# Seven block products for eight in a token mixer's first channel product, for the last two of its five units

## The chip, the cores and the metric

The kernel runs on one core of a Trainium2 chip. The metric is the device time of one execution in microseconds. TensorE (PE) multiplies matrices into PSUM, VectorE (DVE) and ScalarE (ACT) work on SBUF and PSUM, GpSimd (POOL) on SBUF, and the queues of SyncE (SP) and ScalarE issue the DMAs.

## What is computed

```python
def _attn_ref(x, w_r, w_i, b_r, b_i):                # x: 8 x 3008 x 256
    X = np.fft.rfft(x, axis=1)
    Yr = Xr @ w_r - Xi @ w_i + b_r                   # Xr, Xi: real and imaginary part
    Yi = Xr @ w_i + Xi @ w_r + b_i
    ...                                              # both shrunk towards zero by 0.01
    return np.fft.irfft(Y, n=x.shape[1], axis=1)

def _moe_ref(x, w_tok1, w_tok2, w_ch1, w_ch2):
    h = np.maximum(xt @ w_tok1, 0.0) @ w_tok2        # over the 3008 tokens, 256 hidden
    u = x + h.transpose(0, 2, 1)
    h2 = np.maximum(u @ w_ch1, 0.0) @ w_ch2          # over the 256 channels, 1536 hidden
    return u + h2
```

The second function is applied to the result of the first.

## The kernel before

The eight batches are worked through in five units: batch 0, batch 1, and three pairs (`UNITS`, units 0 to 4). For each unit there are two kinds of work.

The spectral steps (`spectral`, `parts`) are the Fourier transform as dense matmuls: a transform of 47 points in 13 groups (`dft47`, `stage1`, which subtract and add pairs of rows first, in `sum_diff`), then for 12 pairs of frequencies a transform of 64 points (`forward`, tiles `px`, `xf`, `xth`, `xtl`), the complex product with the weights and the shrinking (`mix`, tiles `pm`, `z`, `yh`, `yl`), the way back (`inverse`, to `b_d` in DRAM) and the first token product, which adds up in `gp` (`tokens`). `close` rectifies `gp` into `gh` and `gl`, the inputs of the second token product.

The channel steps (`channel`) take a unit's tokens in chunks of 512 columns (the first of a pair's chunks has 384). `make_u` makes u for 470 or 376 tokens at once from `gh`, `gl`, the token weights (`wt2`, loaded by `load_wt2`) and the unit's `b_d` (`load_b2`); `split_u` splits a chunk of u. `first(f)` multiplies one of 12 blocks of 128 hidden values into a PSUM bank `ph` and rectifies it into `hh` and `hlo`; `second(f - 2)`, two blocks later, multiplies them into `po`, which holds the chunk's output through all 12 blocks.

All of these matmuls are made in a form of float32 that TensorE rounds, so each operand is held as a high part and a low part and each product is three matmuls, `mm3`:

```python
        PE.matmul(out, lhsT=wh, rhs=xh, start=start, stop=False)
        PE.matmul(out, lhsT=wh, rhs=xl, start=False, stop=False)
        PE.matmul(out, lhsT=wl, rhs=xh, start=False, stop=stop)
```

`split` makes the two parts: the high one is a copy (ScalarE, or VectorE for u), the low one a subtraction (VectorE, GpSimd in places). PSUM is eight banks: four go round under the tag `w` (`bank`), two belong to `po` and two to `gp`.

The order of the work around the change is written out by hand in the last loop. The channel chunks of unit u are run in turn, and between their blocks the loop takes steps of the spectral generator of unit u + 1, at a pace worked out from two sums of costs: 70.3 us for a batch of spectral steps (`left_s`) and 32.7 us for a channel chunk (`left_c`). At `"end"`, in the last chunk of a unit, what is left of the spectral steps is run. So unit 4's channel has no spectral steps beside it. A scheduler then puts each engine's instructions in order by what is ready in its own model, without changing what waits for what; engines run their queues in order.

Of the kernel before, what the change touches and what calls it, by code (L numbers as in the profile page):

```python
# [10 lines left out]
F32 = mybir.dt.float32  # L11
# [22 lines left out]
NCH = 1  # L34
NF = DF // 128


# [84 lines left out]
def tile_kernel(ctx: ExitStack, tc: tile.TileContext, io):  # L122
# [3 lines left out]
    const = ctx.enter_context(tc.tile_pool(name="const", bufs=1))  # L126
    wk = ctx.enter_context(tc.tile_pool(name="wk", bufs=2))
    dram = ctx.enter_context(tc.tile_pool(name="dram", bufs=1, space=bass.MemoryType.DRAM))
# [55 lines left out]

    def mm3(out, wh, wl, xh, xl, start, stop):
        PE.matmul(out, lhsT=wh, rhs=xh, start=start, stop=False)  # L186
        PE.matmul(out, lhsT=wh, rhs=xl, start=False, stop=False)  # L187
        PE.matmul(out, lhsT=wl, rhs=xh, start=False, stop=stop)  # L188


    f1w = const.tile([120, 3, 128], F32, name="f1")
    f1 = f1w[:, :, :120]
    f1r = const.tile([120, 2, 2, 128], F32R, name="f1r")
    f2 = const.tile([128, 4, 96], F32, name="f2")
# [3 lines left out]
    bias = const.tile([128, 2, C], F32, name="bias")  # L198
    wmh = const.tile([128, 3, 2, C], F32R, name="wmh")
    wml = const.tile([128, 3, 2, C], F32R, name="wml")  # L200
    wc = {}

# [18 lines left out]
    a_d = [dram.tile([128, KH, 512], F32, name=f"a_d{p}") for p in range(2)]  # L221
    b_d = [dram.tile([NSLOT, 96, 512], F32, name=f"b_d{p}") for p in range(2)]

# [177 lines left out]


    def parts(u):
        plain = u == 0
        bs = UNITS[u]
        nb = len(bs)
        w = nb * C
        a, bd = a_d[u % 2], b_d[u % 2]

# [111 lines left out]
        def close():  # L521
            gh = const.tile([128, 2, nb, C], F32R, name="gh", tag="gh")
            gl = const.tile([128, 2, nb, C], F32R, name="gl", tag="gl")
            for j in range(2):
                hv, gv = gh[:, j].rearrange("p b c -> p (b c)"), acc[0][:, j, :w]
                S.activation(out=hv, in_=gv, func=AF.Relu)
                V.scalar_tensor_tensor(out=gl[:, j].rearrange("p b c -> p (b c)"), in0=gv, scalar=0.0, in1=hv.bitcast(F32), op0=ALU.max, op1=ALU.subtract)
            gts[u] = gh, gl

        return SimpleNamespace(**{k: v for k, v in locals().items()})  # L530
# [49 lines left out]
    def begin(sp):  # L580
# [14 lines left out]
        with tc.tile_pool(name="early", bufs=1) as early:  # L595
# [25 lines left out]
            for n in range(NW + KP):  # L621
# [37 lines left out]
                if n in (NC + 9, NC + 10):  # L659
                    f.append(narrow_w2(len(f), early))  # L660
        wc["wk2"] = ctx.enter_context(tc.tile_pool(name="wk2", bufs=2))
        load_b2(0)
# [22 lines left out]
    for u, bs in enumerate(UNITS):  # L685
        total, at = N * len(bs), 0
        widths = [k * TOKS for k in sizes] if u == 0 else [total % CW] + [CW] * (total // CW)
# [21 lines left out]
    def load_wt2(g, pool=None):  # L709
        u, _, s, k = groups[g]  # L710
        cols = slice(s * TOKS, (s + k) * TOKS)
        if u == 0:
            wfs[g] = [load_wide(io["wt2"][0, jt][:, cols], k * TOKS, pool) for jt in range(2)]
        else:
            w = wk.tile([128, 4, 480], F32R, name="wt2", bufs=1)
            DMA.dma_start(out=w[:, :, :k * TOKS].bitcast(F32), in_=wt2_d[:, :, cols])
            wts[g] = w
# [11 lines left out]
    def load_b2(g):  # L729
        u, b, s, k = groups[g]  # L730
        b2 = wc["wk2"].tile([96, SPC, C], F32, name="b2", bufs=1)
        DMA.dma_start(out=b2[:, :k], in_=b_d[u % 2].rearrange("s q w -> q s w")[:, s:s + k, b * C:(b + 1) * C])
        b2s[g] = b2

    def make_u(g):
# [6 lines left out]
        for m in homes:  # L742
            if m not in ufs:
                ufs[m] = wc["wk2"].tile([128, 2, CW], F32, name="uf", bufs=3)
        for ct in range(2):
# [29 lines left out]
    def channel(n):  # L775
# [23 lines left out]
        for f in range(NF + 2):  # L799
# [9 lines left out]
            if after:  # L809
                mine = needs[n + 1]  # L810
                if f == 0 and mine:
                    load_wt2(mine[0])
                if f == 2:
                    if after[0] != u:
                        yield "end"
                    if mine:
                        load_b2(mine[0])
                first_at = 9 if len(mine) == 1 else 6
                for i, g in enumerate(mine):
# [7 lines left out]
                if f == 10:  # L827
                    split_u(n + 1)
            yield (1.37 if f in (0, 1, NF, NF + 1) else 2.73) * cw / CW
        o = wk.tile([128, 2, CW], F32, tag="o", name="o", bufs=3)  # L830
        step = 2 if after else 1
# [7 lines left out]


    def run(gen):
        for _ in gen:
            pass
# [68 lines left out]
```

## Time and profile before

| | |
|---|---|
| three runs | 2445.38, 2449.03 and 2450.14 us, median 2449.03 |
| profiled execution, first to last instruction (its span) | 2442.4 us |
| lowest of the runs less that span | 3.0 us |
| TensorE, VectorE, ScalarE, GpSimd busy | 2420.4, 1103.6, 875.3, 305.2 us |
| granted TensorE clock | 1.00 |

The time of the profiled execution outside its span is not shown apart; the three runs lie 3.0 to 7.7 us above the span. Busy times of TensorE come from matmuls that overlap, so the row of one matmul is longer than the distance to the next one's start.

### The profile page before, as it was taken

The numbers are of one execution on the slowest core, as the hardware profiler recorded it, in microseconds if no ns is written. First come the engines' busy times: TensorE is split into PE (matmuls) and PEld (weight loads), VectorE is DVE, ScalarE is ACT, GpSimd is POOL, SyncE is SP. The second block draws the span as 40 slices with busy tenths as digits, with TensorE's granted clock in tenths as the row PEclk, the third lists the DMA queues.
The fourth block names the chain that finished last, engine by engine and source line by source line (L and its number), as shares of the span: only waits on it lengthen the run. The fifth ranks groups of instructions, "written<-read, shape, count | busy, mean of one in ns | idle before, by whom it ended". The sixth has DMA issues, their size and how long they took to land.

```text
span 2442.4 us, 31613 instructions
## 1 busy us (share of the span) xinstructions
PE 2420.4 (99%) x12848; PEld 2114.3 (87%) x12848; DVE 1103.6 (45%) x1680; ACT 875.3 (36%) x1580; POOL 305.2 (12%) x259
## 2 busy tenths in 40 slices
PE   8999999999999999999999999999999999999999
PEld 7778999988888888888888898888888888888887
DVE  7986655454445444433344353444334333232332
ACT  6764444443333343333333253333333222222221
POOL 0000223122222011111111120111111000000000
PEclk9999999999999999999999999999999999999999
DMA  8864335542324352223322363232321212112110
GB/s 216 254 210 141 102 111 160 167 138 93 100 86 131 112 170 72 60 80 91 89 75 69 98 177 105 68 99 76 93 67 37 70 50 64 59 49 81 37 56 18
DMA packets 143998, 246.07 MB, mean 101 GB/s; under 512 B 10293, under 2 KB 97677, under 8 KB 143853
## 3 DMA queue, kind: packets, MB, share of 16 engines
q1 hardware_dynamic: 114073, 190.57, 26.4%
q10 hardware_dynamic: 29780, 53.49, 7.0%
q8 instruction: 101, 1.65, 0.3%
q14 instruction: 44, 0.36, 0.0%
HBM read 159.74 MB, written 84.28 MB: 100 GB/s over the span
## 4 chain that ended last, share of the span: by engine, by line
PE 93%; DMA 2%; DVE 2%; ACT 1%; SPq 1%; issue 0%; POOL 0%; ACTq 0%; DVEq 0%; POOLq 0%
PE ph L186 10%; PE ph L187 10%; PE ph L188 10%; PE po L188 10%; PE po L186 10%; PE po L187 10%; PE pu L751 5%; PE px L451 3%; PE pm L186 2%; PE pm L188 2%; PE pm L187 2%; PE pu L186 2%; PE pu L187 2%; PE pu L188 2%; PE gp L186 2%; PE gp L188 2%
## 5 line engine op out<-in xcount | busy, mean ns | idle before, releaser
L790 DVE SCALAR_TENSOR_TENSOR hlo<-ph,hh 128x512 fp32r<-128x512 f32 (+4 forms) x588 | 392.0, 667 | 640.0 <-ACT hh L789 635.8
L789 ACT ACTIVATE hh<-ph 128x512 fp32r<-128x512 f32 (+4 forms) x588 | 340.9, 581 | 822.3 <-PE ph L188 820.2
L186 PE MATMUL ph<-uh,w 128*128 128x512 f32 (+4 forms) x1176 | 455.7, 388 | 0.9 <-DVE hlo L790 0.9
L187 PE MATMUL ph<-ul,w 128*128 128x512 f32 (+4 forms) x1176 | 449.1, 382 | 0.0
L186 PE MATMUL po<-hh,w2h 128*128 128x512 f32 (+4 forms) x1176 | 448.5, 381 | 0.0
L188 PE MATMUL ph<-uh,w 128*128 128x512 f32 (+4 forms) x1176 | 448.5, 381 | 0.0
L187 PE MATMUL po<-hlo,w2h 128*128 128x512 f32 (+4 forms) x1176 | 447.9, 381 | 0.0
L188 PE MATMUL po<-hh,w2l 128*128 128x512 f32 (+4 forms) x1176 | 447.8, 381 | 0.0
L188 PEld LDWEIGHTS ph<-uh,w 128*128 128x128 f32 x1176 | 220.8, 188 | 39.5
L187 PEld LDWEIGHTS po<-hlo,w2h 128*128 128x128 f32 x1176 | 220.9, 188 | 38.6
L186 PEld LDWEIGHTS po<-hh,w2h 128*128 128x128 f32 x1176 | 220.8, 188 | 38.5
L188 PEld LDWEIGHTS po<-hh,w2l 128*128 128x128 f32 x1176 | 220.8, 188 | 38.4
L186 PEld LDWEIGHTS ph<-uh,w 128*128 128x128 f32 x1176 | 221.2, 188 | 35.5 <-DVE hlo L790 1.3
L187 PEld LDWEIGHTS ph<-ul,w 128*128 128x128 f32 x1176 | 221.3, 188 | 34.0 <-DVE ul L760 0.2
L140 DVE TENSOR_TENSOR xtl<-xf,xth 128x768 fp32r<-128x768 f32 x84 | 80.5, 958 | 208.7 <-ACT xth L137 208.7
L186 PE MATMUL pm<-wmh,xth 128*128 128x256 f32 x504 | 144.4, 287 | 1.1 <-ACT xth L137 1.1
L758 ACT COPY uf<-pu 128x470 f32<-128x470 f32 (+23 forms) x188 | 62.7, 376 | 228.1 <-PE pu L751 228.1
L140 POOL TENSOR_TENSOR yl<-z,yh 128x512 fp32r<-128x512 f32 x72 | 92.9, 1290 | 408.6 <-ACT yh L137 408.6
L188 PE MATMUL pm<-wmh,xtl 128*128 128x256 f32 x504 | 142.4, 283 | 0.0
L187 PE MATMUL pm<-wml,xth 128*128 128x256 f32 x504 | 142.3, 283 | 0.0
L751 PEld LDWEIGHTS pu<-g,b 96*128 96x128 f32 x1024 | 130.8, 191 | 3.4
L454 POOL TENSOR_TENSOR xf<-xf 128x256 f32<-128x256 f32 x84 | 69.0, 821 | 484.8 <-ACT xf L453 483.3
(130 smaller groups left out, 3216.3 us busy)
## 6 DMA issues: line engine op xcount, KB each, us to landing
wt<-wt_d SPq DMA_DIRECT2D x28, 940.0 KB, 5.6
x<-in_x SPq DMA_DIRECT2D x39, 480.0 KB, 4.4
a<-a_d SPq DMA_DIRECT2D x36, 512.0 KB, 3.8
b_d<-bt ACTq DMA_DIRECT2D x36, 512.0 KB, 3.3
out<-o SPq DMA_DIRECT2D x34, 512.0 KB, 2.8
a_d<-a ACTq DMA_DIRECT2D x36, 480.0 KB, 3.4
wt<-wt_d SPq DMA_DIRECT2D x21, 752.0 KB, 5.2
b<-b_d SPq DMA_DIRECT2D x32, 480.0 KB, 6.3
```

What stands on the lines that cost most here:

```text
L140: lo_eng.tensor_tensor(out=lo, in0=src, in1=hi.bitcast(F32), op=ALU.subtract)
L186: PE.matmul(out, lhsT=wh, rhs=xh, start=start, stop=False)
L187: PE.matmul(out, lhsT=wh, rhs=xl, start=False, stop=False)
L188: PE.matmul(out, lhsT=wl, rhs=xh, start=False, stop=stop)
L451: PE.matmul(pt[:, o:o + 128], lhsT=x, rhs=f2cols(2 * kp + ab), start=True, stop=True)
L454: (V if plain else G).tensor_tensor(out=xf[:, 0], in0=xf[:, 1], in1=xf[:, 2], op=ALU.add)
L751: PE.matmul(pt[:, s * TOKS:(s + 1) * TOKS], lhsT=b2[:, s, cs], rhs=g2[:, 0 if s0 + s == 0 else 1], start=False, stop=s == k - 1)
L758: S.copy(out=ufs[m][:, ct, lo - at:hi - at], in_=pt[:, lo - c0:hi - c0])
L789: S.activation(out=hh, in_=pt, func=AF.Relu)
L790: V.scalar_tensor_tensor(out=hlo, in0=pt, scalar=0.0, in1=hh.bitcast(F32), op0=ALU.max, op1=ALU.subtract)
```

## The change

Units 3 and 4 do the first channel product with seven block products in place of eight. A chunk has 1024 columns there (the first one 896), cut into two halves of 512 (448). The block matrix of weights has two hidden blocks by two blocks of 128 channels, that of u two blocks of channels by two halves. `weigh` makes four sums of weight blocks (`ws`), `sum_u` four sums of the blocks of u (in `t7`), `split_u7` splits the seven right factors (`ub`). `first7` makes the products of one pair of hidden blocks, into four banks: x takes three of them, w two, q and z one each. The results are read out between: what x and w hold after the first and second product is copied to SBUF by ScalarE (`snap`), and VectorE adds q, w and x to the copies. The four rectified blocks wait one pair for `second7`, which adds up both halves' outputs, in the two banks of `po` and the two of `gp`. So `gp` is no longer free for spectral steps beside them: those of units 3 and 4 stand beside unit 2's channel (`BESIDE`). `gh` and `gl` of units 3 and 4 go to DRAM in between (`g_d`), `b_d` has one copy for each unit, and the pools of the spectral steps are closed before the new tiles are opened (`open_seven`, in unit 2's last chunk).

```diff
+SEVEN = (3, 4)
+CW7 = 2 * CW
+BESIDE = {0: [1], 1: [2], 2: [3, 4]}
...
         def close():
-            gh = const.tile([128, 2, nb, C], F32R, name="gh", tag="gh")
-            gl = const.tile([128, 2, nb, C], F32R, name="gl", tag="gl")
+            if u in SEVEN:
+                gh, gl = hl([128, 2, nb, C], "gh"), hl([128, 2, nb, C], "gl")
+            else:
+                ...
             gts[u] = gh, gl
+            if u in SEVEN:
+                for i, g in enumerate(gts[u]):
+                    PUT.dma_start(out=g_d[u][i], in_=g.rearrange("p j b c -> p (j b c)").bitcast(F32))
...
+    def open_seven():
+        spectrum.close()
+        pool = wc["seven"] = ctx.enter_context(tc.tile_pool(name="seven", bufs=1, side="right", reuse_waits="tile"))
+        wc["wt2"] = wc["b2"] = wc["uf"] = pool
+        wc["ws"] = pool.tile([128, NF // 2, 4, 2, 128], F32R, name="ws")
...
+    def sum_u(n):
+        ...
+        b11, b12, b21, b22 = (uf[:, t, k * h:(k + 1) * h] for t in range(2) for k in range(2))
+        ...
+        V.tensor_tensor(out=t1, in0=b12, in1=b11, op=ALU.subtract)
+        V.tensor_tensor(out=t2, in0=b22, in1=t1, op=ALU.subtract)
+        V.tensor_tensor(out=t3, in0=b22, in1=b12, op=ALU.subtract)
+        V.tensor_tensor(out=t4_, in0=b21, in1=t2, op=ALU.subtract)
+        us[n] = uf, (b11, t1, b21, t2, b22, t4_, t3), []
...
+    def first7(n, p):
+        ...
+        product(x, 4, 0)
+        S.copy(out=snap[0], in_=x)
+        product(w, 0, 1)
+        S.copy(out=snap[1], in_=w)
+        product(q, 5, 2)
+        V.tensor_tensor(out=snap[0], in0=q, in1=snap[0], op=ALU.add)
+        product(x, 1, 3, False)
+        S.copy(out=snap[2], in_=x)
+        rectify(0, 0, snap[0])
+        product(w, 3, 4, False)
+        V.tensor_tensor(out=snap[2], in0=w, in1=snap[2], op=ALU.add)
+        rectify(0, 1, snap[2])
+        product(z, 6, 5)
+        S.copy(out=snap[3], in_=z)
+        product(x, 2, 6, False)
+        V.tensor_tensor(out=snap[3], in0=x, in1=snap[3], op=ALU.add)
+        V.tensor_tensor(out=snap[1], in0=x, in1=snap[1], op=ALU.add)
+        rectify(1, 0, snap[3])
+        rectify(1, 1, snap[1])
+        return hs
...
+    def channel7(ns):
+        ...
+        for n in ns:
+            ...
+            for p in range(half):
+                hs = first7(n, p)
+                if behind:
+                    second7(*behind, 0, (0, 1))
+                if p < len(mine):
+                    make_u(mine[p])
+                    ...
+                if behind:
+                    second7(*behind, 1, (0, 1))
+                    if p == 0:
+                        for k in range(2):
+                            finish7(behind[0], k, 2)
+                behind = n, p, hs
+                if after and p == half - 2:
+                    sum_u(after)
+                    for i in range(2):
+                        split_u7(after, i)
+                if after and p == half - 1:
+                    for i in range(2, 7):
+                        split_u7(after, i)
...
     for n, (u, at, cw) in enumerate(chunks):
-        if at == 0 and u + 1 < len(UNITS):
+        if u in SEVEN:
+            channel7(range(n, len(chunks)))
+            break
+        if at == 0:
             if u:
-                sp, done = spectral(u + 1), 0.0
-            left_s = len(UNITS[u + 1]) * 70.3 - done
+                sp, done = chain.from_iterable(spectral(v) for v in BESIDE[u]), 0.0
+            left_s = sum(len(UNITS[v]) for v in BESIDE[u]) * 70.3 - done
```

Up to the start of unit 2's channel every engine has the same instructions in the same order as before. The built order at three places, each with the waits that the instruction itself holds (`Activation` is ScalarE):

TensorE, unit 4's last chunk, before: one hidden block of `first` (`ph`), one of `second` (`po`).

```order
L186 MATMUL ph<-uh,w_949 128x512
L187 MATMUL ph<-ul,w_949 128x512
L188 MATMUL ph<-uh,w_949 128x512
L186 MATMUL ph<-uh,w_949 128x512
L187 MATMUL ph<-ul,w_949 128x512
L188 MATMUL ph<-uh,w_949 128x512
L186 MATMUL po<-hh,w2h 128x512 [waits Activation_49]
L187 MATMUL po<-hlo,w2h 128x512 [waits DVE_49]
L188 MATMUL po<-hh,w2l 128x512
L186 MATMUL po<-hh,w2h 128x512
L187 MATMUL po<-hlo,w2h 128x512
L188 MATMUL po<-hh,w2l 128x512
```

TensorE, unit 4's last chunk, now: the first four products of a pair of hidden blocks, x, w, q and x again (line 192 to 194 is `mm3`).

```order
L192 MATMUL sx<-ub,w_957 128x512 [waits DVE_49]
L193 MATMUL sx<-ub,w_957 128x512
L194 MATMUL sx<-ub,w_957 128x512
L192 MATMUL sw<-ub,ws 128x512 [waits DVE_49]
L193 MATMUL sw<-ub,ws 128x512
L194 MATMUL sw<-ub,ws 128x512
L192 MATMUL sq<-ub,w_957 128x512 [waits Activation_49]
L193 MATMUL sq<-ub,w_957 128x512
L194 MATMUL sq<-ub,w_957 128x512
L192 MATMUL sx<-ub,ws 128x512 [waits Activation_49]
L193 MATMUL sx<-ub,ws 128x512
L194 MATMUL sx<-ub,ws 128x512
```

Between a bank's filling and its next use there were other banks' blocks only; now the second product into x stands 6 matmuls behind the first, and waits for ScalarE's copy of it.

ScalarE, around a chunk border in unit 4, before: `hh` rectifies, `uf` is u copied from PSUM.

```order
L789 ACTIVATE hh<-ph 128x512 [waits DVE_49,PE_49] x12
L758 COPY uf<-pu 128x104 [waits PE_49]
L758 COPY uf<-pu 128x272
L758 COPY uf<-pu 128x104 [waits PE_49]
L758 COPY uf<-pu 128x272
L789 ACTIVATE hh<-ph 128x512 [waits DVE_49,PE_49] x12
```

ScalarE, the last pair of hidden blocks ahead of the last chunk, now: `sn` are the copies out of the banks, `hh` the rectifications, `ub` the high parts of the next chunk's seven factors.

```order
L943 COPY sn<-sx 128x512 [waits PE_49,Activation_49]
L143 CAST ub<-uf 128x512
L945 COPY sn<-sw 128x512 [waits PE_49,Activation_49]
L143 CAST ub<-t_20042 128x512
L143 CAST ub<-uf 128x512 [waits PE_49]
L949 COPY sn<-sx 128x512 [waits PE_49,Activation_49]
L938 ACTIVATE hh_20077<-sn 128x512 [waits DVE_49]
L955 COPY sn<-sz 128x512 [waits PE_49,Activation_49]
L143 CAST ub<-t_20042 128x512
L938 ACTIVATE hh_20085<-sn 128x512 [waits DVE_49]
L143 CAST ub<-t_20042 128x512
L938 ACTIVATE hh_20098<-sn 128x512 [waits DVE_49]
```

The split copies, which VectorE made for u before, stand between the copies for which TensorE waits.

VectorE, around a chunk border in unit 4, before: `hlo` are the low parts, `uh` and `ul` the split of u, `o` the output.

```order
L790 SCALAR_TENSOR_TENSOR hlo<-ph,hh 128x512 [waits Activation_49] x10
L139 CAST uh<-uf 128x1024 [waits Activation_49]
L140 TENSOR_TENSOR ul<-uf,uh 128x1024 [waits DVE_49]
L790 SCALAR_TENSOR_TENSOR hlo<-ph,hh 128x512 [waits Activation_49] x2
L834 TENSOR_TENSOR o<-po,uf 128x1024 [waits DMAHW6_49,PE_49]
```

VectorE, one pair of hidden blocks in unit 4's last chunk, now: the four additions to the copies (`sn`) and the four low parts.

```order
L947 TENSOR_TENSOR sn<-sq,sn 128x512 [waits PE_49,Activation_49]
L952 TENSOR_TENSOR sn<-sw,sn 128x512 [waits PE_49,Activation_49]
L939 SCALAR_TENSOR_TENSOR hlo_20251<-sn,hh_20250 128x512 [waits Activation_49]
L957 TENSOR_TENSOR sn<-sx,sn 128x512 [waits PE_49,Activation_49]
L939 SCALAR_TENSOR_TENSOR hlo_20259<-sn,hh_20258 128x512 [waits Activation_49]
L958 TENSOR_TENSOR sn<-sx,sn 128x512
L939 SCALAR_TENSOR_TENSOR hlo_20272<-sn,hh_20271 128x512 [waits Activation_49]
L939 SCALAR_TENSOR_TENSOR hlo_20276<-sn,hh_20275 128x512 [waits Activation_49]
```

Four additions that read the banks q, w and x (twice) stand now among the four low parts of a pair.

More of the change, by code (lines that the diff above doesn't have):

```diff
@@ new lines, in split_u7, with left @@
+    def split_u7(n, i):
+        h = chunks[n][2] // 2
+        _, srcs, done = us[n]
+        ub = wc["seven"].tile([128, 2, CW], F32R, name="ub", bufs=9)
+        split(ub[:, 0, :h], ub[:, 1, :h], srcs[i], S, V)
+        done.append(ub)
+    def left(p, i):
+        w1 = wc["w1"]
+        if i < 4:
+            return [wc["ws"][:, p, i, k] for k in range(2)]
+        f, ct = {4: (0, 0), 5: (0, 1), 6: (1, 1)}[i]
+        return [w1[:, k, ct, (2 * p + f) * 128:(2 * p + f + 1) * 128] for k in range(2)]
@@ new lines, in first7, with product, rectify @@
+    def first7(n, p):
+        h = chunks[n][2] // 2
+        ubs = us[n][2]
+        x, w, q, z = (bank(k)[:, :h] for k in ("sx", "sw", "sq", "sz"))
+        snap = [wc["tail"].tile([128, CW], F32, tag="sn", name="sn", bufs=6)[:, :h] for _ in range(4)]
+        hs = {}
+        def product(out, a, i, start=True):
+            ub = ubs[i]
+            mm3(out, *left(p, a), ub[:, 0, :h], ub[:, 1, :h], start, True, not start)
+        def rectify(f, k, t):
+            hh = wc["tail"].tile([128, CW], F32R, tag="hh7", name="hh7", bufs=8)[:, :h]
+            hlo = wc["tail"].tile([128, CW], F32R, tag="hlo7", name="hlo7", bufs=8)[:, :h]
+            S.activation(out=hh, in_=t, func=AF.Relu)
+            V.scalar_tensor_tensor(out=hlo, in0=t, scalar=0.0, in1=hh.bitcast(F32), op0=ALU.max, op1=ALU.subtract)
+            hs[f, k] = hh, hlo
+        product(x, 4, 0)
[18 more added lines that the diff above has]
+        return hs
@@ new lines, in tile_kernel, with second7, finish7 @@
+    pos = {}
+    def second7(n, p, hs, f, order):
+        h = chunks[n][2] // 2
+        if n not in pos:
+            pos[n] = [ps1.tile([128, 2, 512], F32, tag=tag, name="po") for tag in ("po", "gp")]
+        for k in order:
+            hh, hlo = hs[f, k]
+            for ct in range(2):
+                cs = slice(ct * 128, (ct + 1) * 128)
+                mm3(pos[n][k][:, ct, :h], wc["w2h"][:, 2 * p + f, cs], wc["w2l"][:, 2 * p + f, cs], hh, hlo, p + f == 0, 2 * p + f == NF - 1)
+    def finish7(n, k, step):
+        u, at, cw = chunks[n]
+        h = cw // 2
+        uf = us[n][0]
+        for c in range(0, 2, step):
+            cs = slice(c, c + step)
+            o = uf[:, cs, k * h:(k + 1) * h]
+            V.tensor_tensor(out=o, in0=pos[n][k][:, cs, :h], in1=o, op=ALU.add)
+            for b, bi in enumerate(UNITS[u]):
+                lo, hi = max(at + k * h, b * N), min(at + (k + 1) * h, (b + 1) * N)
+                if lo < hi:
+                    DMA.dma_start(out=outv[bi][:, cs, lo - b * N:hi - b * N], in_=uf[:, cs, lo - at:hi - at])
```

118 lines of the change are left out of this document (92 added, 26 removed).

## The prediction

> **What bounds the kernel now.** I read the head of the page first, then the chain that ended last, then the busy time by stage, then what TensorE waited for, then single matmuls. The head and one line of the chain:
>
> ```profile
> span 2442.4 us, 31613 instructions
> PE 2420.4 (99%) x12848; PEld 2114.3 (87%) x12848; DVE 1103.6 (45%) x1680; ACT 875.3 (36%) x1580; POOL 305.2 (12%) x259
> PE 93%; DMA 2%; DVE 2%; ACT 1%; SPq 1%; issue 0%; POOL 0%; ACTq 0%; DVEq 0%; POOLq 0%
> ```
>
> TensorE is busy for 99% and is 93% of the chain; the other engines stand below half. The stages, by the windows view: the start, unit 1's channel beside unit 2's spectral steps, unit 2's beside unit 3's, unit 3's beside unit 4's, unit 4's alone (columns: stretch, length, busy time and instructions of each engine, granted clock, DMA share, GB/s):
>
> ```profile
> 0.00:200.00 200.00, 185.97 (x1029) 157.41 (x1030) 166.24 (x343) 131.39 (x240) 2.74 (x6) 1.00 0.78 226
> 433.00:783.00 350.00, 348.05 (x1941) 308.05 (x1941) 169.71 (x241) 143.47 (x250) 85.06 (x71) 1.00 0.38 114
> 785.00:1365.00 580.00, 580.00 (x3040) 503.88 (x3039) 244.56 (x338) 196.12 (x351) 85.89 (x73) 1.00 0.32 95
> 1370.00:1955.00 585.00, 585.00 (x3062) 508.00 (x3061) 240.33 (x333) 194.38 (x348) 78.88 (x69) 1.00 0.29 87
> 2010.00:2430.00 420.00, 420.00 (x2011) 357.21 (x2010) 126.04 (x168) 94.87 (x181) 0.00 (x0) 1.00 0.17 52
> ```
>
> From 785 on TensorE never pauses: what it waited for between 785 and 2440 gives no row at all. In 433 to 783 it waited three times:
>
> ```profile
> PE p L186 <- ACT a L257: 0.9, 1, 0.9
> PE px L451 <- DMA a<-a_d: 0.7, 1, 0.7
> PE p L187 <- DVE xl L140: 0.3, 1, 0.3
> ```
>
> So in units 3 and 4 the time is the number of matmuls by the distance between their starts, and whatever makes TensorE wait is added whole. Distances and the relay to the other engines come from the timeline in unit 4 (start, duration, engine, line); the second fence is from unit 4's 384-wide chunk:
>
> ```profile
> 2106.89 0.39 PE L186 MATMUL ph<-uh,w 128*128 128x512 f32 x1
> ...
> 2108.02 0.39 PE L188 MATMUL ph<-uh,w 128*128 128x512 f32 x1
> ...
> 2108.45 0.60 ACT L789 ACTIVATE hh<-ph 128x512 fp32r<-128x512 f32 x1 [0.76 <-PE ph L188]
> ...
> 2109.08 0.69 DVE L790 SCALAR_TENSOR_TENSOR hlo<-ph,hh 128x512 fp32r<-128x512 f32 x1 [0.67 <-ACT hh L789]
> ...
> 2109.61 0.39 PE L186 MATMUL po<-hh,w2h 128*128 128x512 f32 x1
> ```
>
> ```profile
> 1997.95 0.33 PE L186 MATMUL ph<-uh,w 128*128 128x384 f32 x1
> ...
> 1998.99 0.33 PE L186 MATMUL ph<-uh,w 128*128 128x384 f32 x1
> ```
>
> From 2106.89 to 2109.61 are 12 starts: 2.72 / 12 = 0.2267 us for each 512-wide matmul, not the 0.39 of its row, since they overlap. Six 384-wide ones take 1.04: 0.173 each. A 448-wide one lies halfway: 0.200. ScalarE starts 0.43 us after the start of the last matmul of a group (2108.02 to 2108.45), VectorE 0.03 us after ScalarE's end.
>
> **What is removed.** A product of two blocks is three matmuls (high by high, high by low, low by high). For each pair of hidden blocks and 1024 tokens there were 8 products in the first channel step, now 7: 3 matmuls less, 6 times in a chunk, 18 per chunk. Units 3 and 4 have five chunks of 1024 and one of 896 (halves of 448) each. Ten chunks x 18 x 0.2267 = 40.8 us, two x 18 x 0.200 = 7.2 us: **48.0 us** of TensorE's time. The new cut itself is free: 512 + 384 columns cost 0.2267 + 0.173 = 0.400, twice 448 the same. The second channel step and the products that make u keep their matmuls.
>
> The Trainium skill (TensorE: Matmul & The Clock Gate, Back-to-back issue gap) gives N / 2.4 + 2.5 ns between warm matmuls, 215.8 ns at 512 and 189.2 at 448; by that, as an estimate, 45.7 us would go. The rows show 226.7, so I keep 48.0.
>
> **What is added in each period.** A period is one pair of hidden blocks: 21 matmuls of the first step and 24 of the second, 45 x 0.2267 = 10.2 us. The new work between them is four copies out of PSUM on ScalarE and four additions on VectorE, beside the four rectifications and four splits that were there. Prices, from the groups of one shape each:
>
> ```profile
> L453 ACT COPY xf<-px 128x512 f32<-128x512 f32 x96 | 56.4, 588 | 111.4 <-PE px L451 109.0 <-issue 1.5 <-ACT bt L505 0.7
> L789 ACT ACTIVATE hh<-ph 128x512 fp32r<-128x512 f32 x456 | 272.1, 598 | 705.0 <-PE ph L188 703.5 <-DVE et L140 0.9 <-ACT et L137 0.3
> L137 ACT CAST yh<-z 128x512 fp32r<-128x512 f32 x72 | 44.7, 621 | 39.6 <-DVE z L488 39.6
> L790 DVE SCALAR_TENSOR_TENSOR hlo<-ph,hh 128x512 fp32r<-128x512 f32 x456 | 314.1, 690 | 568.7 <-ACT hh L789 564.7
> L481 DVE TENSOR_TENSOR z<-pm,z 128x512 f32<-128x512 f32 x96 | 66.1, 689 | 13.7 <-PE pm L188 11.2
> L488 DVE TENSOR_TENSOR z<-z 128x512 f32<-128x512 f32 x84 | 58.1, 692 | 2.7
> L834 DVE TENSOR_TENSOR o<-po,uf 128x1024 f32<-128x1024 f32 x37 | 45.3, 1223 | 66.2 <-PE po L188 66.2
> ```
>
> VectorE: 8 x 0.69 = 5.5 us in 10.2; ScalarE: 4 x 0.588 + 4 x 0.598 = 4.7. Neither becomes the bound. What counts is order, because the bank of x is read and then added to while TensorE stands in line. A product lasts 0.68; from its start to the moment ScalarE may read it are 2 x 0.2267 + 0.43 = 0.88. The products run x 0, w 0.68, q 1.36, x 2.04, w 2.72, z 3.40, x 4.08 to 4.76. The first copy of x runs 0.88 to 1.48, and the second product into x wants it at 2.04; the copy of w ends at 2.16, wanted at 2.72; the second copy of x ends at 3.52, wanted at 4.08. Each has 0.56 us to spare. VectorE's eight steps, in the built order, run from 2.24 to 8.43 (the addition into the last sum, which frees the bank of x, ends at 7.05), and the next period wants VectorE at 12.44. The second step uses what the period before has made. I take **nothing** for a steady period. Lower bound nothing, since an added wait brings no time; upper bound: 72 periods x 0.3, the shortest wait TensorE shows, is 22 us. It is nearer to the stage from 785 on, where no wait shows.
>
> When u is made, its two banks are those that q and w left at 2.93 and 4.29, wanted at 4.76 or later: nothing. The next `wt2` is asked for as soon as the last group is done, a whole period (over 10 us) before its use, and lands in 5.6 (row below).
>
> **Chunk borders.** Seven splits of the next chunk's halves and sums share ScalarE and VectorE with the last period; five of their copies (0.621) stand between the copies out of PSUM. In that built order ScalarE runs: copy of x to 1.48, a split copy to 2.12, copy of w to 2.74 (wanted at 2.72), two split copies to 3.98, copy of x to 4.58 (wanted at 4.08). TensorE waits 0.07 + 0.48 = 0.55 us; 11 borders: **6 us**. Bounds: 0, and 11 x 5 x 0.621 = 34 if all five split copies were exposed. The four sums and seven lower halves (11 x 0.69) and the two additions of 1.22 at the end make VectorE's chunk 33.1 + 7.6 + 2.4 = 43 us in 61 without u's products: covered.
>
> **Unit 2's stage.** The spectral steps of unit 4, matmuls unchanged, stand now behind those of unit 3 beside unit 2's channel. VectorE in the third stretch: by the kernel's own pace, 70.3 us a batch, its 580 us hold 140 of spectral steps and so 440 of channel; at unit 4's rate (126.04 / 420 = 0.30) the channel takes 132, so one unit's spectral steps 112. Unit 2's stage becomes 440 + 280 = 720 us with 132 + 224 = 356 on VectorE, 49%: the density of the stretch 433 to 783 (169.71 / 350 = 48%), which did the same kind of work and lost 1.95 us. Twice that: **4 us**. Lower bound 0 (third stretch), upper 2 units x 13 groups x 0.9 = 23. The matmuls behind such a wait are the channel's own, so it costs its length.
>
> **The entry.** Behind the last spectral step the pools are opened anew, so the `wt2` of unit 3's first group may be asked for only when the last token product and the `out` of the chunk before it are through: 0.43 + 1.22 + 0.40 (its issue) = 2.1 us after that chunk's last matmul. It is queued on SP, and what follows it there is `b2`.
>
> ```profile
> 2106.98 0.40 SPq L838 DMA_DIRECT2D out<-o  x1
> wt<-wt_d SPq DMA_DIRECT2D x28, 940.0 KB, 5.6
> b<-b_d SPq DMA_DIRECT2D x32, 480.0 KB, 6.3
> ```
>
> It lands at 7.7, `b2` at 8.8; TensorE has 48 matmuls, 10.9 us, before it needs the first. The fetched `gh`, `gl` (512 KB each) are asked for some 25 us ahead. The sums of the weights (three times 2 x 1.22 + 4 x 0.42, about 12 us of VectorE in a chunk of some 43) have till the chunk's end. **1 us** for the first, narrower period; bounds 0 and 6.3, one whole load. The four writes of `gh`, `gl` to DRAM hold ScalarE for an issue each (0.40 on SP), in stretches where it is busy for 4 tenths: nothing. The end is as it was: two additions and a store behind the last matmul.
>
> **Sum.** 2442.4 - 48.0 + 6 + 4 + 1 = 2405.4 us of span. The runs are 2445.38 to 2450.14 with a median 6.6 us above the profiled span; with that, **2412 us**, 1.5% below 2449.03.
>
> **Rivals.**
> *Unit 2's stage stalls.* Unit 4's first transform starts with two of the four `hl` buffers still holding unit 3's `gh`, `gl`, and its groups stand closer together than unit 3's do today. At the upper bound it costs 23 rather than 4: 2431 us. For it: in 433 to 783 both waits of `p` are in just this transform. Against: there too it was 1.2 us in all.
> *The copies come late.* If ScalarE's copies end later than 0.56 us after my timetable, every one of 72 periods loses the excess e; the 37 us of gain are gone at e = 37 / 72 = 0.51, so at copies 1.07 us late, nearly two more of them in line. With e = 0.7: 2412 + 50 = 2462, slower. For it: ScalarE obeys a strict order, with a rectification that waits on VectorE between. Against: it is through at 7.7 of 10.2 us, and the row of 598 repeats 456 times. With e near 0.5 the time is the same.
> *The clock falls.* Short waits between groups on four banks in turn might throttle TensorE; at half speed each microsecond of matmuls costs another, and 37 us of such work, 4% of units 3 and 4, would undo the gain. Twice that much gives 2412 + 74 = 2486 us. Against: in the first 200 us TensorE paused for 14 us and the granted clock stayed 1.00. The Trainium skill (TensorE: Matmul & The Clock Gate, A second HAM failure mode: psum-queue depth-cycling) describes such a fall; the first stretch does not bear it out here.
>
> **How the numbers follow.** The forecast has a chance of 0.72, unit 2's stalls 0.13, late copies 0.13 (0.07 of it the same, 0.06 slower), the clock 0.02. About 0.2%, 4.9 us, is what a measurement of this kernel can tell. Faster 0.72 + 0.13 = 0.85, same 0.07, slower 0.08. The range begins at 2397 (no cost at all, 2401, and the 3.6 us by which the fastest run lies below the median) and ends at 2436 (the stalled stage, 2431, and a border cost doubled); it leaves out the last two rivals and a little of the others.
>
> **What would show it.** Right: 216 records less on TensorE, no wait of `sx`, `sw` on ScalarE inside a chunk, waits of about 0.5 us at the third product into x at borders only, units 3 and 4 shorter by some 42 us together, unit 2's stage 140 us longer. Wrong: such waits in every period; waits of `p` on `xl` or `a` over 1 us around the start of unit 4's transform; a granted clock below 1.00 behind 1500; TensorE waiting for `wt2` at the entry.

## The result, and the profile after

Four runs gave 2418.50, 2420.28, 2420.67 and 2421.42 us, median 2420.48, against 2447.47 us (2445.38 to 2450.14, four runs) for the kernel before. The ratio is 0.9889, with a 95% interval of 0.9875 to 0.9903: 1.1% faster. Forecast were 2412 us, 1.5% faster, and 2397 to 2436. So sign and range held, while a quarter of the expected 37 us did not come: 27.0 did.

The head of the page and a line of its chain:

```profile
span 2418.5 us, 32134 instructions
PE 2392.1 (99%) x12632; PEld 2079.9 (86%) x12632; DVE 1321.4 (55%) x2070; ACT 1082.1 (45%) x1931; POOL 308.4 (13%) x259
PE 93%; DVE 3%; DMA 2%; ACT 1%; SPq 1%; issue 0%; POOL 0%; ACTq 0%; DVEq 0%; POOLq 0%
```

TensorE has 12632 records where it had 12848, the 216 of the forecast, and is still the bound. ScalarE went from 36% to 45%, VectorE from 45% to 55%, and neither took over. Next the windows view (columns as before: stretch, length, busy time and instructions of each engine, granted clock, DMA share, GB/s): two short pairs of stretches, then unit 2's stage, unit 3's and unit 4's.

```profile
485.00:497.00 12.00, 9.31 (x46) 7.33 (x44) 6.68 (x6) 6.03 (x10) 5.37 (x3) 1.00 0.87 258
497.00:502.00 5.00, 4.91 (x16) 4.30 (x17) 2.48 (x3) 4.32 (x8) 0.00 (x0) 0.66 0.47 123
1185.00:1197.00 12.00, 10.06 (x43) 7.58 (x42) 8.43 (x10) 5.92 (x9) 3.80 (x3) 1.00 0.89 285
1197.00:1202.00 5.00, 4.89 (x16) 3.45 (x14) 4.96 (x5) 3.52 (x6) 3.24 (x3) 0.66 0.56 169
785.00:1365.00 580.00, 576.29 (x3110) 500.89 (x3109) 285.96 (x389) 237.94 (x410) 135.78 (x111) 1.00 0.41 124
1575.00:1990.00 415.00, 415.00 (x1990) 352.52 (x1989) 231.12 (x361) 197.65 (x362) 0.00 (x0) 1.00 0.20 60
2000.00:2410.00 410.00, 410.00 (x1945) 347.29 (x1945) 225.75 (x347) 191.26 (x347) 0.00 (x0) 1.00 0.17 51
```

From 1575 on TensorE is busy without a break, and what it waited for behind 1555 gives no row, as in the kernel before. In unit 2's stage VectorE stands at 49% (285.96 / 580), as forecast. New are the stretches from 497 and from 1197, where the mean clock is 0.66: each holds 3.41 us at half clock, right behind a pause. The waits of TensorE in unit 2's stage (engine, line, waited for, total, times, longest):

```profile
PE p L193 <- DVE xl L146: 2.5, 3, 1.7
PE pm L192 <- ACT xth L143: 1.1, 2, 0.7
```

The main loss gives no row of that view. It is seen in the starts of the timeline: the first matmul of two periods of unit 4, 45 matmuls apart, with the copies of ScalarE in between.

```profile
2185.20 0.40 PE L192 MATMUL sx<-ub,w 128*128 128x512 f32 x1
...
2186.16 0.59 ACT L943 COPY sn<-sx 128x512 f32<-128x512 f32 x1 [3.59 <-PE sx L194]
...
2186.85 0.59 ACT L945 COPY sn<-sw 128x512 f32<-128x512 f32 x1
...
2187.30 0.40 PE L192 MATMUL sx<-ub,ws 128*128 128x512 f32 x1
...
2191.68 0.39 PE L193 MATMUL po<-hlo,w2h 128*128 128x512 f32 x1
2191.91 0.39 PE L194 MATMUL po<-hh,w2l 128*128 128x512 f32 x1
...
2195.54 0.40 PE L192 MATMUL sx<-ub,w 128*128 128x512 f32 x1
```

A period lasts 2195.54 - 2185.20 = 10.34 us, not 45 x 0.2267 = 10.20. The copies are in time as in the timetable: that of x ends at 2186.75 (2186.16 + 0.59), and TensorE comes back to x at 2187.30, 0.55 us later. But the nine matmuls from 2185.20 to 2187.30 take 2.10 / 9 = 0.233 us each, while those of the second step run at 0.227 again (2191.68 to 2191.91). A matmul that starts 6 or 7 ns late gives no row in the waits view.

### The profile page after: what moved, and what is told of

Its sections match the earlier page's. It is cut to its first block, busy times and chain, and to the rows that moved or that the text cites. A ratio compares the mean times of both kernels' runs of the same rounds, so it can differ in the third digit from the quotient of the medians.

```text
span 2418.5 us, 32134 instructions
## 1 busy us (share of the span) xinstructions
PE 2392.1 (99%) x12632; PEld 2079.9 (86%) x12632; DVE 1321.4 (55%) x2070; ACT 1082.1 (45%) x1931; POOL 308.4 (13%) x259
## 4 chain that ended last, share of the span: by engine, by line
PE 93%; DVE 3%; DMA 2%; ACT 1%; SPq 1%; issue 0%; POOL 0%; ACTq 0%; DVEq 0%; POOLq 0%
PE po L192 10%; PE po L194 10%; PE po L193 10%; PE ph L192 5%; PE ph L193 5%; PE ph L194 5%; PE pu L772 5%; PE px L465 3%; PE pm L192 2%; PE pm L194 2%; PE pm L193 2%; PE sx L192 2%; PE sx L194 2%; PE sx L193 2%; PE pu L192 2%; PE pu L194 2%
## 5 line engine op out<-in xcount | busy, mean ns | idle before, releaser
L811 DVE SCALAR_TENSOR_TENSOR hlo<-ph,hh 128x512 fp32r<-128x512 f32 (+4 forms) x300 | 196.7, 656 | 249.6 <-ACT hh L810 247.8
L810 ACT ACTIVATE hh<-ph 128x512 fp32r<-128x512 f32 (+4 forms) x300 | 171.4, 572 | 285.4 <-PE ph L194 280.7
L192 PE MATMUL ph<-uh,w 128*128 128x512 f32 (+4 forms) x600 | 230.9, 385 | 0.9 <-DVE hlo L811 0.9
L193 PE MATMUL ph<-ul,w 128*128 128x512 f32 (+4 forms) x600 | 228.1, 380 | 0.0
L194 PE MATMUL ph<-uh,w 128*128 128x512 f32 (+4 forms) x600 | 227.5, 379 | 0.0
L938 ACT ACTIVATE hh<-sn 128x512 fp32r<-128x512 f32 (+1 forms) x288 | 180.7, 627 | 58.0 <-DVE sn L958 37.9
L939 DVE SCALAR_TENSOR_TENSOR hlo<-sn,hh 128x512 fp32r<-128x512 f32 (+1 forms) x288 | 193.8, 673 | 7.0 <-ACT hh L938 0.6
L947 DVE TENSOR_TENSOR sn<-sq,sn 128x512 f32<-128x512 f32 (+1 forms) x72 | 48.9, 680 | 199.3 <-PE sq L194 184.6
L943 ACT COPY sn<-sx 128x512 f32<-128x512 f32 (+1 forms) x72 | 41.6, 578 | 230.0 <-PE sx L194 229.9
L779 ACT COPY uf<-pu 128x470 f32<-128x470 f32 (+20 forms) x164 | 61.2, 406 | 175.3 <-PE pu L772 174.9
```

What stands on the lines that cost most here:

```text
L192: PE.matmul(out, lhsT=wh, rhs=xh, start=start, stop=False, skip_group_check=more)
L193: PE.matmul(out, lhsT=wh, rhs=xl, start=False, stop=False, skip_group_check=more)
L194: PE.matmul(out, lhsT=wl, rhs=xh, start=False, stop=stop, skip_group_check=more)
L779: S.copy(out=ufs[m][:, ct, lo - at:hi - at], in_=pt[:, lo - c0:hi - c0])
L810: S.activation(out=hh, in_=pt, func=AF.Relu)
L811: V.scalar_tensor_tensor(out=hlo, in0=pt, scalar=0.0, in1=hh.bitcast(F32), op0=ALU.max, op1=ALU.subtract)
```

## The experiments

**Three theories on the slow matmuls, first round.** Most distances between 512-wide matmuls on `ub` are 231 to 236 ns with weights in `w1` and 224 to 236, on average 231, with weights in `ws`; the five behind them stand 229 to 235 apart. (1) The waits come true late and take TensorE's lead. (2) Groups of three, each with a wait and a signal, cost by themselves. (3) It is the operands.

*The move alone* (`e1_eight`), groups of six and no copies:

```diff
-        product(x, 4, 0)
-        S.copy(out=snap[0], in_=x)
-        ...
+        for (f, k), out in zip(((0, 0), (0, 1), (1, 0), (1, 1)), (x, w, q, z)):
+            for t in range(2):
+                ...
+                mm3(out, wc["w1"][:, 0, t, fs], wc["w1"][:, 1, t, fs], ub[:, 0, :h], ub[:, 1, :h], t == 0, t == 1)
+            rectify(f, k, out)
```

> The move alone: units 3 and 4 keep the chunks of 1024 columns, their place behind the moved spectral steps, the order of products and second step of the change, but the first product is made from eight block products again, six matmuls into each of four banks, rectified straight out of the bank; the sums of weights and of u, the copies out of the banks and the additions are left out. In the changed kernel matmuls of the first product and the five behind them stand 231 to 236 ns apart instead of 226.7, about 0.13 us in a period, 8 us in 60 periods. Theory 1 (TensorE's instructions run ahead of their turn, and a wait that comes true only about half a microsecond before its turn takes this lead away) and theory 2 (a group of only three matmuls with a wait and a signal of its own costs some ns, whenever its wait came true) both expect 226.7 again here, so 2420.5 + 48.0 - 8 = 2460 us. Theory 3 (it is the operands: the ub tiles, or the wider chunk) expects 231 to 236 still and 2468 us. What stands above the 2447.5 of before is the price of the move, 8 to 13 us; had the move cost nothing it would be 2447 to 2449.

Measured: 2472.10 us (2471.15 to 2479.53), ratio to before 1.0105 (1.0089 to 1.0122). The 24 matmuls on `ub` stood 233 ns apart; ten of them:

```profile
2196.16 0.39 PE L192 MATMUL sw<-ub,w 128*128 128x512 f32 x1
...
2198.49 0.39 PE L193 MATMUL sq<-ub,w 128*128 128x512 f32 x1
```

Only theory 3 expected that. So the move by itself costs some 23 us, of which some 12 are the excess of the matmuls on `ub` over 226.7 and 200.0 ns. The seven products bring 2472.1 - 2420.5 = 51.6 us: 48.0 are the matmuls, and much of the rest is that fewer of them are slow.

*Waits far ahead* (`e2_spread`), the order of one period changed:

```diff
         product(z, 6, 5)
         S.copy(out=snap[3], in_=z)
+        between[0]()          # second step of the pair before, first half; u's matmuls
         product(x, 1, 3, False)
         ...
+        between[1]()          # second half
         product(x, 2, 6, False)
```

> The same products in another order: x, w, q and z first, then half of the second step of the pair before (with u's matmuls, where there are any), then the second products into x and w, the other half of the second step, and last the third product into x. Each copy out of a bank is then through 2.6 us or more before the bank is wanted again, where it was 0.56. The groups stay at three matmuls, each with its wait and its signal. Theory 1 (waits that come true late take TensorE's lead away) expects 226.7 ns throughout and 8 us less, less about 1 us at the very end where the last third product has no cover: 2413 us. Theory 2 (short groups cost by themselves) expects 231 to 236 ns in the groups as before, and 2420 to 2422 us.

Measured: 2421.12 us, 0.9897 (0.9881 to 0.9914): nothing gained. Most matmuls on `ub` with `w1` as weights still stood 231 to 235 ns apart, such as these six, 1.40 us in all:

```profile
2184.07 0.39 PE L192 MATMUL sq<-ub,w 128*128 128x512 f32 x1
...
2185.47 0.40 PE L192 MATMUL po<-hh,w2h 128*128 128x512 f32 x1
```

Theories 1 and 2 have both fallen, the second with the kernel above.

**The addresses.** In the built programs the tiles on the left side of SBUF that matmuls read lie at multiples of 64 bytes, while the right side ends at byte 229344 of a partition, 32 past such a multiple. The change put the spectral steps' pools and the new one on the right. So `ub`, `ws` and the spectral tiles lie 32 bytes off, `w1`, `w2h`, `hh7` at multiples of 64. In the kernel before, all of these were at multiples of 64. (A remainder here is what an address leaves when it is divided by 64.)

*One small tile* (`e6_aligned`) at the pool's upper end moves `ub`, `ws` and that pool's other tiles; *all tiles* (`e7_all`) adds the line of `none`; *all 32 off* (`e8_shift`) does the opposite to the kernel before:

```diff
+        pad = wc["seven"].tile([128, 8], F32, name="pad")
+        V.memset(pad, 0.0)
...
-        none = pool.tile([rows, 1], F32, name="none")
+        none = mid.tile([rows, 1], F32, name="none")
...
-    sc = const.tile([128, 16], F32, name="sc")
+    sc = const.tile([128, 8], F32, name="sc")
```

> The changed kernel with one tile of 32 bytes more, at the upper end of the pool that units 3 and 4's channel works in, so that its other tiles (ub, ws, t7, uf, wt2) lie 32 bytes lower and ub and ws begin at addresses that 64 divides, as uh and ul do in the kernel before; the work and its order stay. Groups of six and waits that come true early both left the matmuls on ub 231 to 236 ns apart, so theories 1 and 2 have fallen. Theory 3, now in this form: 512-wide matmuls whose moving operand begins 32 bytes off a multiple of 64 lose some 5 ns each, and the five behind them too. It expects 226.7 ns on ub, 60 periods x 0.13 = 8 us less, 2412 us. Theory 4 (something else of the ub tiles, such as high and low part in one tile) expects no change, 2420 us.

> The kernel before this one, and the tile none (32 bytes with its padding) moved from the left side to the upper end of the pool mid, so that the spectral steps' tiles (xh, xth, yh, yl, wt, et), which the change had put on the right side 32 bytes off, lie at multiples of 64 too. Theory 3 expects 512-wide matmuls of the spectral steps (p, pi, gp) to lose their 3 to 5 ns, about 3 us in unit 2's stage: 2409 us. Theory 4 expects 2412 us at the least, nothing from this step.

> The other way round: the kernel before, with the tile sc made 32 bytes smaller (the part left out is not used), so that nearly all tiles behind it, uh, ul, hh, hlo and the weights among them, lie 32 bytes off a multiple of 64. Theory 3: some 6,300 matmuls of 512 columns lose 3.5 to 5 ns each, 22 to 32 us, 2470 to 2480 us. Theory 4: no change, 2447 to 2449 us.

Measured: 2413.29 us, 0.9855 (0.9841 to 0.9869), with the tile; 2408.82 us, 0.9838 (0.9825 to 0.9851), with all tiles; and 2446.95 us, 0.9993 (0.9982 to 1.0003), with nearly everything 32 bytes off. The timeline of `e6_aligned`, first matmuls of two periods:

```profile
2182.53 0.39 PE L192 MATMUL sx<-ub,w 128*128 128x512 f32 x1
2182.76 0.39 PE L193 MATMUL sx<-ub,w 128*128 128x512 f32 x1
...
2192.73 0.39 PE L192 MATMUL sx<-ub,w 128*128 128x512 f32 x1
```

10.20 us, what 45 x 0.2267 makes: the 7 to 8 us are back, and `e7_all` brings 4.5 more. But the third kernel refutes the theory's wording: a common offset costs nothing. What remains is that weights and moving operand begin at *different* remainders of 64.

That holds for 9 of the 21 matmuls on `ub` in a period of the changed kernel, those with `w1`. The other 12 have `ws`, which lies 32 off as `ub` does; they and the first five of the second step are slow as neighbours of a change of remainder. Of the 7.5 us by which units 3 and 4 are shorter in the trace of `e6_aligned`, 3.9 lie on matmuls with `w1` and 3.6 on the others, nearly all of them such neighbours. The distances of `e7_all` show 2.8 of its 4.5 us, nearly all on matmuls whose own operands had agreed before too, but whose neighbours lay at the other remainder.

*Weights apart* (`e10_apart`), the kernel before with `w1`, `w2h`, `w2l` and what else lies between the two tiles 32 bytes off, and the rest back in place:

```diff
-    sc = const.tile([128, 16], F32, name="sc")
+    sc = const.tile([128, 8], F32, name="sc")
...
+            pad = const.tile([128, 8], F32, name="pad")
+            V.memset(pad, 0.0)
```

> The kernel before with the tile sc 32 bytes smaller and a tile of 32 bytes behind the channel's weights: w1, w2h and w2l lie 32 bytes off a multiple of 64 (as in the kernel where nearly everything lay so, and which ran as fast as before), and uh, ul, hh and hlo lie at multiples of 64, as before. Theory 3 in its first form has fallen with that kernel. Theory 3b: a matmul is slow where its weights and its moving operand begin at different remainders of 64 (0 and 32), which fits the changed kernel (ub at 32, w1 at 0: 231 to 236 ns; aligned: 226.7). It expects some 5,400 matmuls of 512 columns to stand 5 to 6.6 ns further apart: 27 to 36 us more than before, 2475 to 2484 us. Theory 3c: it is the change of the moving operands' remainder from one group to the next; here all of the channel's are at 0, and it expects 2447 to 2450 us.

Measured: 2478.38 us, 1.0122 (1.0105 to 1.0139): 31.6 us more, in the middle of what theory 3b expects; 3c, taken as the only cause, expects none. Unit 4's timeline, `e10_apart`, then `e8_shift`:

```profile
2104.61 0.39 PE L187 MATMUL ph<-ul,w 128*128 128x512 f32 x1
2104.85 0.40 PE L188 MATMUL ph<-uh,w 128*128 128x512 f32 x1
...
2106.71 0.40 PE L187 MATMUL po<-hlo,w2h 128*128 128x512 f32 x1
2106.95 0.39 PE L188 MATMUL po<-hh,w2l 128*128 128x512 f32 x1
```

```profile
2110.66 0.39 PE L188 MATMUL ph<-uh,w 128*128 128x512 f32 x1
2110.89 0.39 PE L186 MATMUL ph<-uh,w 128*128 128x512 f32 x1
...
2115.64 0.39 PE L186 MATMUL ph<-uh,w 128*128 128x512 f32 x1
2115.87 0.39 PE L187 MATMUL ph<-ul,w 128*128 128x512 f32 x1
```

Ten matmuls from 2104.61 to 2106.95 are 0.234 us each with the operands apart; 23 from 2110.66 to 2115.87 are 0.2265 with both 32 off. The same program, but for one tile of 32 bytes and the instruction that fills it, and 1.3% of the time.

Two limits. In the built programs the two addresses of the quick 512-wide matmuls agree in their remainder of 512 as well, and those of the slow ones differ by 32 more, so these runs don't single out 64. And the loss shows at 512 and 448 columns only: in `e10_apart`, matmuls of 256 and 470 columns with their operands apart were no slower than in the kernel before (118 against 120 ns, 211 against 214).

**Unit 2's stage.** The timeline of the changed kernel at its longest wait:

```profile
1192.02 1.05 ACT L143 CAST xh<-sd 120x1024 fp32r<-120x1024 f32 x1
...
1193.67 0.87 PE L192 MATMUL p<-xh,f1r 120*128 120x512 f32 x3
1193.87 1.23 DVE L871 TENSOR_TENSOR o<-po,uf 128x1024 f32<-128x1024 f32 x1 [3.27 <-PE po L194]
1195.01 2.35 DVE L146 TENSOR_TENSOR xl<-sd,xh 120x1024 fp32r<-120x1024 f32 x2
...
1196.27 0.50 PE L193 MATMUL p<-xl,f1r 120*128 120x512 f32 x1 [1.74 <-DVE xl L146]
```

`xh` was there at 1193.07, and VectorE was idle for 3.27 us: it could have made `xl`. But the addition at the chunk's end stood ahead of it in VectorE's queue, waiting for the last matmul into `po`. So TensorE waited for a split that waited for TensorE. Is it this place, or VectorE's density? The pace of the spectral steps moves the place:

```diff
-            left_s = sum(len(UNITS[v]) for v in BESIDE[u]) * 70.3 - done
+            left_s = sum(len(UNITS[v]) for v in BESIDE[u]) * 70.3 * (1.03 if u == 2 else 1.0) - done
```

with 1.03 in `e4_pace`, and 0.98 together with all tiles in place in `e9_all_pace`.

> The changed kernel with one number changed: the pace at which the spectral steps of units 3 and 4 are taken beside unit 2's channel is 3% higher, so that unit 4's first transform starts some 12 us earlier. In the changed kernel TensorE waits 1.9 us there for a split that VectorE could have made, but which stands in VectorE's queue behind the addition at a chunk's end, and the 3.4 us behind it run at half clock: 3.6 us in all. Theory A (it is the place against the chunk's end): no wait over 1 us in this stage, no stretch at half clock there, about 2417 us. Theory B (it is the density of VectorE's work, near half of the stage): 2 to 4 us of waits at other places, 2419 to 2422 us.

> The kernel with all tiles at multiples of 64, and the pace of the spectral steps beside unit 2's channel 2% lower, so that unit 4's first transform, which now starts 9 us ahead of a chunk's end, starts some 8 us later, about at its end. With 3% more the waits in this stage rose to about 15 us instead of falling: theory B's prices were too low as well. Theory A (the place against the chunk's end, where VectorE's addition of 1.22 us stands ahead of the splits): waits in this stage below 2 us, no half clock, 2404 us. Theory B (density): as many waits as in the changed kernel or more, 2408 to 2415 us.

Measured: 2427.65 us (0.9918, 0.9903 to 0.9933) and 2407.13 us (0.9843, 0.9824 to 0.9863). Waits in this stage of the first and of the second:

```profile
PE p L193 <- DVE xl L146: 4.0, 3, 2.0
PE p L192 <- ACT a L265: 3.9, 1, 3.9
PE p L192 <- ACT xh L143: 1.1, 2, 0.6
PE pm L192 <- ACT xth L143: 0.6, 2, 0.3
```

```profile
PE p L193 <- DVE xl L146: 2.0, 4, 0.8
PE pm L194 <- DVE xtl L146: 1.0, 2, 0.5
PE pm L192 <- ACT xth L143: 0.6, 2, 0.3
```

VectorE's work is the same in the changed kernel and these two, and the waits are 3.6, 9.6 and 3.6 us: at one density the place makes 6 us, but neither expectation was met. 3% more made it far worse, with three steps at half clock behind the waits, which A did not expect. With 2% less no wait is over 0.8 us and no stretch at half clock follows, yet the sum of waits did not fall below 2 us. Against the kernel with all tiles the 1.7 us are too little to tell apart. What the best place is stays open.

**What a pause costs.** Pauses put into unit 4's channel of the kernel before:

```diff
+            if u == 4 and cw == CW and f in (3, 8):
+                ...
+                    G.tensor_tensor(out=ul[:, 0, :c], in0=uf[:, 0, :c], in1=uh[:, 0, :c].bitcast(F32), op=ALU.subtract)
```

> The kernel before with 22 pauses of TensorE put into unit 4's channel: at two places of each 512-wide chunk GpSimd makes the first half of ul again (the same values, in steps of 1.29 us), 5.2 to 8.2 us of it, while TensorE has about 5 us of other matmuls: pauses of some 0.3 to 3.3 us. In the changed kernel two pauses, of 2.6 and 1.9 us, were each followed by 3.4 us at half the clock, and in the kernel before one of 1.05 us was not. If pauses do it, those below 1 us leave the clock at 1.00, those of 2 us and more are followed by 3.4 us at half clock, and each of these loses 1.7 us beyond the pause itself; about 22 x 1.5 + 11 x 1.7 = 50 us more than before, 2500 us. If the stretches at half clock have another cause, the clock stays at 1.00 in most of unit 4 whatever the pause, and it is about 2480 us.

Measured, in one run: 2586.26 us. The pauses came out at 3.5 to 5.4 us of extra distance, not 0.3 to 3.3, since TensorE had fewer other matmuls at hand than I had thought. By the windows view, one of them, what follows it, and the stretch around another one:

```profile
2139.00:2143.30 4.30, 0.15 (x1) 0.00 (x0) 0.00 (x0) 0.00 (x0) 4.07 (x4) 0.98 0.00 0
2143.30:2146.60 3.30, 3.02 (x7) 2.47 (x8) 0.00 (x0) 0.48 (x1) 0.23 (x1) 0.51 0.00 0
2155.00:2165.00 10.00, 6.38 (x29) 4.91 (x28) 1.61 (x3) 1.20 (x2) 5.83 (x5) 1.00 0.01 2
```

The clock's record changes only on a grid of 3.413 us. At full clock, each grid step with 2.26 us of pause or more (21 of them) was followed by a step at half clock, and none with 2.00 or less was: the pause at 2158 is 3.8 us long, but falls 1.95 and 1.84 us into two steps, and nothing follows. In the changed kernel 1.9 us were enough once (the step from 1193.9), and at the same place in `e1_eight`, `e6_aligned` and `e7_all`. A step at half clock was itself followed by a second one where 0.66 us or more of pause fell into it (9 of the 21), and by full clock where it was 0.46 or less. The Trainium skill (TensorE: Matmul & The Clock Gate, What's actually happening) tells of a free-running window of 3413 ns and a rule that pauses above some 3.4 us count (HAM oscillation — how this bites in real kernels); the window agrees with the grid here, while about 2 us of pause within one sufficed.

## Why the prediction came out right

The terms in the profiled executions, 2442.4 to 2418.5 us of span. The sums of distances beyond (columns + 32) / 2.4 ns, a formula that fits 226.7 at 512 columns, 173.3 at 384 and 120.0 at 256, are worked out from all records of TensorE. "Addresses" are operands or neighbours at another remainder.

| term | forecast | found |
|---|---|---|
| matmuls removed | -48.0 | -48.0 |
| steady period | 0 (0 to 22) | +7.5, addresses; +1.4, 448 columns |
| chunk borders | +6 | +0.5 |
| unit 2's stage | +4 (0 to 23) | +3.6 waits, +1.7 half clock, +2.0 addresses |
| entry | +1 | no wait |
| the part with the same order, to 828 us | 0 | +4.2 to 534 us, +1.1 addresses behind it |
| not assigned | | +2.1 |
| sum | -37.0 | -23.9 |

- *Matmuls removed*: as forecast. By the rule of the Trainium skill (TensorE: Matmul & The Clock Gate, Back-to-back issue gap), which gives it for a single matmul's gap, it would have been an estimated 45.7 us; the records bear out the rows.
- *Steady period*: the step that failed. "Nothing", because no wait shows. No wait did show, and the copies were 0.55 us ahead as worked out; but the price of a matmul, 0.2267, was read from a kernel whose operands began at like remainders of 64, and taken over for new tiles whose addresses the prediction did not ask for. The new cut was not free either: 448-wide matmuls stand 202.6 ns apart in `e6_aligned`, not 200.0.
- *Chunk borders*: mis-sized by a factor of twelve. ScalarE in a last period of unit 3:

```profile
1693.42 0.62 ACT L143 CAST ub<-uf 128x512 fp32r<-128x512 f32 x1
1693.94 0.59 ACT L945 COPY sn<-sw 128x512 f32<-128x512 f32 x1
1694.42 0.63 ACT L143 CAST ub<-t 128x512 fp32r<-128x512 f32 x1
1694.94 0.63 ACT L143 CAST ub<-uf 128x512 fp32r<-128x512 f32 x1
1695.46 0.60 ACT L949 COPY sn<-sx 128x512 f32<-128x512 f32 x1
...
1696.17 0.45 PE L192 MATMUL sx<-ub,ws 128*128 128x512 f32 x1
1696.46 0.40 PE L193 MATMUL sx<-ub,ws 128*128 128x512 f32 x1
```

  The order is the one that was forecast, but the rows overlap: starts are 0.48 to 0.52 apart, not 0.6. The third product into x starts its second matmul at 1696.46, 0.06 late, in place of 0.48. I had made this correction for TensorE and not for ScalarE. (The forecast's own times, 2.74 for 2.72 and 4.58 for 4.08, make 0.02 + 0.48 = 0.50 us, not 0.07 + 0.48; that is 0.5 us in 11 borders.) The Trainium skill (ScalarE: Activation LUTs, What ACT_TABLE_LOAD costs) says that `ACTIVATE`s back to back overlap by about 93 ns, and these rows, casts and copies, agree with 0.10 to 0.11.
- *Unit 2's stage*: the rival was right in place, unit 4's first transform, and the price, 7.3 us, lies between. A wait of `p` on `xl` over 1 us there was named as a sign of being wrong; it came, with 1.7. What was missing is that a pause of 1.9 us is paid nearly twice.
- *The same code, 5.3 us slower*: 4.2 us of it had come by 534 us. The execution of before that I summed against had no stretch at half clock there; this one had three ahead of 502 us, the last of them (from 497 in the windows above) behind a longer wait, which was 0.9 us before:

```profile
PE p L192 <- ACT a L265: 2.5, 1, 2.5
```

  That is no part of the change: in the eleven traces one and the same matmul of this part starts at 534.1 to 541.2 us, and the kernel before alone, its tiles moved or not, has 534.5 to 539.2. The other 1.1 us is part of it: from there the next 1600 matmuls, the same in all, take 290.0 to 290.1 us in five traces with the spectral steps' operands at their neighbours' remainder, and 291.1 in the five with them 32 bytes off the channel's. The forecast's median also took 6.6 us for what lies around the span; here it is 1.8 (2420.28 for the profiled run), and 2.0 in the later runs of the kernel before, so its profile was of a quick execution. The two slips, 5.3 and 4.8 us, nearly cancel.
- *Late copies, falling clock*: neither came in units 3 and 4, where the clock stayed at 1.00.

So the forecast was right by its largest term. That the rest came out as near as it did was luck: a border 5.5 us too dear stood in for a pace 9 us too cheap.

## What to carry to other kernels

Where TensorE never waits, its time is count times pace, and the pace is a measured thing of its own: when tiles move in memory, compare the distance between starts in two traces, not only the waits. Let the weights and the moving operands of wide matmuls that stand together begin at like addresses (here at one remainder of 64 bytes), above all where pools grow from both ends of memory; it was worth 11.7 us here, beside the 27.0 that the whole change had brought. And work out an engine's timetable from the distances between its starts, since the rows of ScalarE overlap as those of TensorE do.

## What the runs showed of the hardware

- 512-wide matmuls in this form of float32, each with its own weights, start 226.7 ns apart when both operands begin at the same remainder of 64 bytes (0 or 32) and mostly 231 to 235 when one is at 0 and the other at 32 (`e10_apart`, 233 on average); other remainders were not tried. After a change of remainder about five are slow whose own operands agree (229 to 235 in the changed kernel's second step), and after narrow matmuls some six (228 to 231 in the kernel before, the first 315). One small tile made smaller and one added moved the kernel before by 31.6 us.
- At 512, 384 and 256 columns the distance is (columns + 32) / 2.4 ns; 448-wide matmuls took 202.6 in place of 200.0 in `e6_aligned`, with their operands at one remainder.
- Half clock follows about 2 us of pause within one step of a fixed grid of 3.41 us, lasts one step, or two if the pause goes on in it, and costs half of each step, 1.7 us, beyond the pause.
- Two versions beat both kernels: all tiles at multiples of 64, 2408.82 us (ratio to before 0.9838), and this with the pace 2% lower, 2407.13 us (0.9843, 0.9824 to 0.9863), which are not told apart.
